# Twenty-four probability scalings of an attention kernel go from VectorE to GpSimd

## Chip, cores and metric

The kernel runs on one core of a Trainium2 chip. The metric is device time in microseconds, as the median of several executions. The engines are named as in the profile: PE is TensorE (matrix multiplication), DVE is VectorE, ACT is ScalarE, POOL is GpSimd, and SP is the engine that issues the DMAs.

## What is computed

The reference is an attention block with a cache of keys and values and with both projections. There are 8 batches of 112 query rows, 32 heads of width 192, and 512 cached positions; the model width is 640, and all arrays are bf16.

```python
B, Sq, D = 8, 112, 640
H, Sk, Dh = 32, 512, 192
q = (x @ wq).reshape(B, Sq, H, Dh).transpose(0, 2, 1, 3)
scores = jnp.einsum("bhqd,bhkd->bhqk", q, k_cache) * (Dh ** -0.5)
p = softmax(scores, axis=-1)
o = jnp.einsum("bhqk,bhkd->bhqd", p, v_cache)
return o.transpose(0, 2, 1, 3).reshape(B, Sq, H * Dh) @ wo
```

The softmax divides each row of exponentials by its sum. The kernel does this division as a multiplication by the reciprocal of the sum, and this multiplication is what the change is about.

## The kernel before

**Tiling.** The 32 heads are worked in 4 rounds of 8, and a round goes through the 8 batches. For one batch a round takes two steps of 4 heads, so there are 64 steps, numbered n = 0 to 63. Within a step the four heads are called i = 0 to 3. The score matrix of one head has 112 rows (on the partitions) and 512 columns.

**One step.** A step passes through these operations. The names are those in the order lists; the lines are those of the profile.

- `Q` (L720, PE; its copy `evQ` at L146 on ACT) makes the projected queries of a group of batches, and `qc` (L761 and L762, DVE) copies parts of them from SBUF to SBUF to where the second half of the array needs them.
- `KT` (L672, PE) transposes the keys of the first batches through PSUM, and `evK` copies them out, one half on ACT (L146) and one on DVE (L147).
- `Sm` and `St` (L773, PE) multiply queries and keys into PSUM banks 0 to 3. They can start only when the `smax` of the step before have emptied these banks.
- `smax` (L830, DVE), once per head, scales the scores, copies them from PSUM to SBUF and keeps the row's minimum of the negated scores. There are three buffers, so `smax` also waits for the `exp` of three heads earlier.
- `exp` (L835, ACT), once per head, makes the exponentials in bf16 in `p_sb` and their row sums.
- `rc` (L847, DVE), once per pair of heads, takes the reciprocal of two row sums.
- `norm` (L839), once per head, multiplies the 112 x 512 bf16 values of `p_sb` in place by the reciprocal. It reads and writes SBUF only. Before the change all 256 of them are on DVE.
- `PT` (L874, PE) transposes the four scaled matrices of the step. It waits for all four `norm`. `evPT` copies the result out, one half on ACT (L146) and the other on DVE (L147).
- `PVt` and `PVm` (L906 and L918, PE) multiply by the values, `evPV` (L146, ACT) copies the result out.
- `O` (L940, PE) multiplies by the output weights, and `oacc` (L954 and L955, DVE) collects it.

**Order.** Nothing is scheduled at run time. Each engine has a list of operations written out by hand (`ORDER_PE`, `ORDER_ACT`, `ORDER_DVE`, `ORDER_POOL`, `ORDER_SP`), and it works through its list strictly in that order. `Plan.run` (lines 35 to 50) emits for each operation the waits on the other operations that it depends on, by counting semaphores: each engine has one, and an operation waits until the count of the engine that produces its input has reached the place of the producer in that engine's list. An operation's engine is the one in whose list its name stands (`number`, lines 23 to 33). So to move an operation it is enough to take its name from one list and to put it into another:

```python
def norm(e, k=k):
    return e.tensor_scalar(p_sb[:, k, :], p_sb[:, k, :], rinv[:, k:k + 1], None, op0=ALU.mult)
...
add("DVE", ("norm", n, i), [("rc", n, j)], norm)
```

`rc` of step n waits for the `norm` of step n - 2, since both use the same reciprocals' place. Heads 0 and 1 depend on the first `rc` of the step (j = 0), heads 2 and 3 on the second (j = 1).

The steps overlap deeply: while one step's scores are made, the step before is scaled and transposed, and an earlier one is multiplied by its values. In the early steps there is additional work: the keys of the first seven batches are transposed on PE and copied out by ACT and DVE, and two groups of queries are projected. Later keys come already transposed by DMA.

`ORDER_POOL` is empty before the change. GpSimd makes the identity matrix at the start (lines 1156 to 1160) and then has nothing to do.

Of the kernel before, what the change touches and what calls it, by code (L numbers as in the profile page):

```python
# [52 lines left out]
def build_mha_kernel(nc, x, k_cache, v_cache, wq, wo, out):  # L53
# [33 lines left out]
    with ExitStack() as es:  # L87
# [145 lines left out]
        def pv_all(n):  # L233
# [191 lines left out]
            ('smax', 1, 3), ('rc', 0, 1), ('evK', 2, 3, 1), ('norm', 0, 2), ('evK', 1, 1, 1), ('evK', 2, 3, 0),  # L425
            ('norm', 0, 3), ('qc', 3), ('evK', 1, 0, 0), ('evK', 1, 3, 1), ('norm', 0, 1), ('norm', 0, 0), ('rc', 1, 0),
            ('evK', 2, 2, 1), ('evK', 2, 0, 1), ('evK', 2, 0, 0), ('smax', 2, 0), ('smax', 2, 2), ('rc', 1, 1),
            ('norm', 1, 1), ('smax', 2, 1), ('norm', 1, 0), ('norm', 1, 3), ('norm', 1, 2), ('smax', 2, 3), ('qc', 4),
            ('evPT', 0, 1), ('smax', 3, 0), ('smax', 3, 1), ('rc', 2, 0), ('rc', 2, 1), ('evPT', 1, 1), ('norm', 2, 2),
            ('evK', 3, 0, 1), ('norm', 2, 0), ('smax', 3, 2), ('smax', 3, 3), ('norm', 2, 1), ('rc', 3, 0),  # L430
            ('evK', 3, 3, 1), ('norm', 2, 3), ('qc', 5), ('smax', 4, 0), ('smax', 4, 1), ('qc', 6), ('norm', 3, 0),
            ('smax', 4, 2), ('smax', 4, 3), ('evPT', 2, 1), ('rc', 3, 1), ('rc', 4, 0), ('norm', 3, 2), ('norm', 4, 1),
            ('norm', 3, 1), ('norm', 3, 3), ('smax', 5, 0), ('evK', 3, 1, 1), ('evPT', 3, 1), ('smax', 5, 1),
            ('smax', 5, 2), ('smax', 5, 3), ('rc', 5, 0), ('rc', 4, 1), ('evK', 3, 2, 1), ('norm', 4, 2), ('smax', 6, 0),
            ('evK', 4, 1, 1), ('smax', 6, 1), ('evK', 4, 2, 1), ('norm', 4, 0), ('evK', 4, 0, 1), ('norm', 4, 3),
            ('evK', 4, 3, 1), ('qc', 8), ('qc', 7), ('rc', 5, 1), ('norm', 5, 2), ('evPT', 4, 1), ('smax', 6, 2),
            ('smax', 6, 3), ('norm', 5, 1), ('evK', 5, 1, 1), ('norm', 5, 3), ('norm', 5, 0), ('smax', 7, 0),
            ('evPT', 5, 1), ('smax', 7, 2), ('rc', 6, 0), ('rc', 6, 1), ('smax', 7, 1), ('smax', 7, 3), ('qc', 9),
            ('norm', 6, 1), ('rc', 7, 0), ('norm', 6, 2), ('norm', 6, 3), ('norm', 6, 0), ('evK', 5, 3, 1), ('smax', 8, 0),
            ('smax', 8, 1), ('smax', 8, 2), ('evPT', 6, 1), ('evK', 5, 0, 1), ('rc', 7, 1), ('smax', 8, 3),  # L440
            ('evK', 5, 2, 1), ('norm', 7, 0), ('norm', 7, 3), ('norm', 7, 1), ('norm', 7, 2), ('smax', 9, 0),
            ('smax', 9, 1), ('rc', 8, 0), ('qc', 10), ('evPT', 7, 1), ('evK', 6, 2, 1), ('rc', 8, 1), ('smax', 9, 2),
            ('norm', 8, 1), ('smax', 9, 3), ('qc', 11), ('norm', 8, 3), ('smax', 10, 0), ('smax', 10, 1), ('norm', 8, 0),
            ('norm', 8, 2), ('rc', 9, 0), ('evK', 6, 3, 1), ('evK', 6, 0, 1), ('smax', 10, 2), ('evPT', 8, 1), ('rc', 9, 1),
            ('norm', 9, 3), ('qc', 12), ('norm', 9, 0), ('norm', 9, 2), ('norm', 9, 1), ('rc', 10, 0), ('smax', 10, 3),
            ('evK', 6, 1, 1), ('evPT', 9, 1), ('norm', 10, 0), ('smax', 11, 0), ('norm', 10, 1), ('smax', 11, 1),
            ('smax', 11, 2), ('rc', 10, 1), ('smax', 11, 3), ('norm', 10, 2), ('norm', 10, 3), ('rc', 11, 0), ('qc', 13),
            ('smax', 12, 0), ('evPT', 10, 1), ('norm', 11, 1), ('rc', 11, 1), ('smax', 12, 1), ('smax', 12, 2),
            ('norm', 11, 2), ('smax', 12, 3), ('norm', 11, 0), ('rc', 12, 0), ('norm', 11, 3), ('qc', 14), ('oacc', 0, 0),
            ('smax', 13, 0), ('norm', 12, 0), ('smax', 13, 2), ('evPT', 11, 1), ('smax', 13, 1), ('rc', 12, 1),  # L450
            ('smax', 13, 3), ('oacc', 0, 4), ('smax', 14, 2), ('norm', 12, 3), ('norm', 12, 1), ('smax', 14, 0),
            ('smax', 14, 1), ('qc', 15), ('norm', 12, 2), ('oacc', 0, 1), ('rc', 14, 0), ('smax', 14, 3), ('qc', 16),
            ('evPT', 12, 1), ('rc', 13, 0), ('norm', 14, 1), ('rc', 13, 1), ('norm', 13, 3), ('oacc', 0, 2), ('rc', 14, 1),
            ('norm', 13, 2), ('norm', 13, 0), ('oacc', 0, 3), ('norm', 14, 2), ('norm', 13, 1), ('smax', 15, 0),
# [96 lines left out]
            ('norm', 63, 3), ('evPT', 62, 1), ('oacc6', 1), ('evPT', 63, 1), ('oacc6', 2), ('oacc6', 0), ('oaccL', 0),  # L551
            ('oaccL', 1)]
        ORDER_POOL = [
]
        ORDER_SP = [
# [608 lines left out]
def bass_standalone__mha_block_cached__near_ridge_kernel(  # L1164
    nc: bass.Bass,
    x: bass.AP,
    k_cache: bass.AP,
    v_cache: bass.AP,
    wq: bass.AP,
    wo: bass.AP,  # L1170
    out: bass.AP,
):
    return build_mha_kernel(nc, x, k_cache, v_cache, wq, wo, out)
# [28 lines left out]
```

## Time and profile before

| what | value |
|---|---|
| median of 3 runs | 438.99 us |
| the three runs | 438.66, 438.99, 440.42 us |
| the profiled execution's own time | 438.76 us |
| its span | 437.0 us |
| granted TensorE clock, mean | 0.995 |
| PE busy | 423.3 us (97%) |
| PE weight loads busy | 290.2 us (66%) |
| DVE busy | 363.1 us (83%) |
| ACT busy | 343.7 us (79%) |
| POOL busy | 0.7 us (0%) |
| DMA traffic | 122.04 MB, mean 279 GB/s |

The span is the time from the first to the last instruction of the profiled execution; its own time holds another 1.76 us around it. PE stands at 97% because its busy time counts pipelined matrix multiplications up to their modelled ends, so PE at 97% is an engine that nearly always has an instruction under way, not one at its peak rate. The shares are means over the whole run. In a row of the timeline the columns are the start in the span, the time taken, the engine, the line, the instruction, its output and input, and how many were merged; a bracket at the end gives the idle time of the engine just before, and who ended it. In a row of the groups the figures behind the first bar are the busy time in us and the mean in ns of one instruction, those behind the second bar the idle time before them.

### The profile page before, as it was taken

How to read it: one execution, taken by the hardware profiler on the slowest of the kernel's cores; microseconds unless marked ns; L12 is line 12 of the kernel's file. 1: busy time of each engine (PE TensorE's matmuls, PEld its weight loads, DVE VectorE, ACT ScalarE, POOL GpSimd, SP SyncE). 2: the span in 40 equal slices, each digit the busy share in tenths (PEclk: the TensorE clock that was granted, in tenths of full speed). 3: DMA queues.
4: the chain of work that ended last, by engine and by line, in shares of the span. 5: the costliest groups of instructions: out<-in, count | busy, mean ns of one | idle time of the engine just before them, and what ended most of it. 6: DMA issues, size and time to landing. Idle time of an engine off the chain costs nothing.

```text
span 437.0 us, 16234 instructions
## 1 busy us (share of the span) xinstructions
PE 423.3 (97%) x6805; PEld 290.2 (66%) x6805; DVE 363.1 (83%) x1169; ACT 343.7 (79%) x770; POOL 0.7 (0%) x6
## 2 busy tenths in 40 slices
PE   7999979999999999999999999999999999999996
PEld 4666756667677566666667666666766666576896
DVE  1479987989699889898999887889799878999872
ACT  2699979998579787988878777887878856985774
POOL 0000000000000000000000000000000000000000
PEclk9999999999999999999999999999999999999999
DMA  7998999999999999999999999999999999999972
GB/s 255 366 354 289 331 358 287 213 289 342 238 288 286 283 256 257 362 263 255 308 240 237 337 255 256 364 352 287 232 242 376 204 247 349 289 252 252 239 201 82
DMA packets 222858, 122.04 MB, mean 279 GB/s; under 512 B 165312, under 2 KB 222784, under 8 KB 222784
## 3 DMA queue, kind: packets, MB, share of 16 engines
q1 hardware_dynamic: 222784, 120.99, 106.6%
q8 instruction: 54, 0.88, 0.8%
q14 instruction: 20, 0.16, 0.1%
HBM read 78.22 MB, written 1.15 MB: 182 GB/s over the span
## 4 chain that ended last, share of the span: by engine, by line
PE 85%; DVE 7%; ACT 4%; DMA 2%; issue 1%; SPq 0%; DVEq 0%; ACTq 0%
PE ps L940 19%; PE ps L720 19%; PE ps L773 18%; PE ps L918 12%; PE ps L906 7%; PE ps L874 5%; DVE s_sb L830 4%; PE ps L672 2%; ACT p_sb L835 2%; DMA wq_sb<-in_wq_dram 2%; DVE p_sb L839 1%; ACT kt L146 1%; PE ps L973 1%; ACT qr L146 1%; DVE pT_sb L147 1%
## 5 line engine op out<-in xcount | busy, mean ns | idle before, releaser
L835 ACT ACTIVATE p_sb<-s_sb,nmx 112x512 bf16<-112x512 f32 x256 | 183.0, 718 | 32.8 <-DVE s_sb L830 25.6
L830 DVE TENSOR_SCALAR_CACHE_REDUCE s_sb<-ps 112x512 f32<-112x512 f32 x256 | 169.2, 683 | 23.3 <-PE ps L773 19.1
L720 PE MATMUL ps<-xT_sb,wq_sb 128*128 128x448 bf16 x480 | 103.2, 356 | 3.1 <-DMA wq_sb<-in_wq_dram 2.1
L773 PE MATMUL ps<-kt,qr 128*128 128x256 bf16 (+1 forms) x512 | 95.6, 273 | 1.1 <-ACT oT_sb L146 0.4
L940 PE MATMUL ps<-oT_sb,wo_sb 128*128 128x448 bf16 (+1 forms) x480 | 93.3, 341 | 0.3 <-DVE pT_sb L147 0.2
L773 PE MATMUL ps<-kt,qh 128*128 128x256 bf16 (+1 forms) x512 | 87.5, 272 | 0.0
L839 DVE TENSOR_SCALAR p_sb<-p_sb,rinv 112x512 bf16<-112x512 bf16 x256 | 81.2, 346 | 1.5
L720 PEld LDWEIGHTS ps<-xT_sb,wq_sb 128*128 128x128 bf16 x480 | 43.1, 98 | 41.9 <-DMA wq_sb<-in_wq_dram 2.8
L940 PEld LDWEIGHTS ps<-oT_sb,wo_sb 128*128 128x128 bf16 x480 | 44.3, 98 | 35.4 <-DVE pT_sb L147 0.8
L146 ACT ACTIVATE oT_sb<-ps 128x672 bf16<-128x672 f32 x64 | 46.1, 725 | 22.3 <-PE ps L918 21.7
L773 PEld LDWEIGHTS ps<-kt,qr 128*128 128x128 bf16 (+1 forms) x512 | 44.3, 96 | 25.7 <-issue 14.3
L146 ACT ACTIVATE qr<-ps 128x448 bf16<-128x448 f32 x96 | 49.7, 541 | 12.8 <-PE ps L720 12.1
L146 ACT ACTIVATE pT_sb<-ps 128x768 bf16<-128x768 bf16 x59 | 47.0, 800 | 10.3 <-PE ps L874 10.2
L918 PE MATMUL ps<-pT_sb,vt 128*128 128x112 bf16 x944 | 54.9, 213 | 0.0
L918 PEld LDWEIGHTS ps<-pT_sb,vt 128*128 128x128 bf16 x944 | 47.4, 98 | 4.1
L835 ACT ACTIVATION_READ_ACCUMULATOR p_sb<-s_sb,nmx 112x1 f32 x256 | 49.7, 194 | 0.0
L773 PEld LDWEIGHTS ps<-kt,qh 128*128 128x128 bf16 (+1 forms) x512 | 43.9, 96 | 6.1
L147 DVE COPY pT_sb<-ps 128x1024 bf16<-128x1024 bf16 x59 | 40.2, 682 | 2.4 <-PE ps L874 1.3
L874 PE MATMUL ps<-ident,p_sb 64*128 64x64 bf16 (+1 forms) x1888 | 37.4, 186 | 0.9 <-DVE p_sb L839 0.5
L874 PEld LDWEIGHTS ps<-ident,p_sb 64*128 64x128 bf16 (+1 forms) x1888 | 33.2, 94 | 6.9 <-DVE p_sb L839 2.6
L906 PE MATMUL ps<-pT_sb,vt 128*64 128x112 bf16 x944 | 32.8, 215 | 1.4 <-DVE s_sb L830 0.5
L906 PEld LDWEIGHTS ps<-pT_sb,vt 128*64 128x64 bf16 x944 | 25.5, 110 | 12.2 <-issue 3.4
(53 smaller groups left out, 228.2 us busy)
## 6 DMA issues: line engine op xcount, KB each, us to landing
vt<-in_v_cache_dram SPq DMA_DIRECT2D x64, 768.0 KB, 6.7
wo_sb<-in_wo_dram SPq DMA_DIRECT2D x8, 960.0 KB, 8.2
wq_sb<-in_wq_dram SPq DMA_DIRECT2D x14, 480.0 KB, 5.7
wo_sb<-in_k_cache_dram SPq DMA_DIRECT2D x6, 768.0 KB, 7.1
accT<-in_k_cache_dram SPq DMA_DIRECT2D x6, 768.0 KB, 7.2
vt<-in_k_cache_dram SPq DMA_DIRECT2D x2, 768.0 KB, 8.5
out_dram<-xT_sb SPq DMA_DIRECT2D x8, 140.0 KB, 2.5
wq_sb<-in_wq_dram SPq DMA_DIRECT2D x1, 960.0 KB, 7.5
```

Source lines behind the costliest of these rows:

```text
L146: return e.activation(dst, src, ACTF.Copy)
L147: return e.tensor_copy(dst, src)
L672: ends = [e.transpose(psb[:, bank + t, y * 64:(y + 1) * 64], kn[i][64 * t:64 * t + 64, 2 * p + u, c * 128:(c + 1) * 128], ident[64 * t:64 ...
L720: mm = e.matmul(ps[:, bank, 0:SG], w, v, start=(dc == 0), stop=(dc == DC - 1))
L773: return e.matmul(ps[:, 2 * j + odd, hs], q, ktb[j][lo:hi, :, blk, h * 128:(h + 1) * 128], start=first, stop=last, skip_group_check=True)
L830: return e.tensor_scalar(s_sb[:, a, :].rearrange("p (e c) -> p e c", e=2), ps[0:SQ, 2 * j:2 * j + 2, h * 256:(h + 1) * 256], -scale, None, ...
L835: return e.activation(p_sb[:, k, :], s_sb[:, a, :], ACTF.Exp, bias=nmx[:, k:k + 1], scale=-1.0, accum_out=rsum[:, k:k + 1])
L839: return e.tensor_scalar(p_sb[:, k, :], p_sb[:, k, :], rinv[:, k:k + 1], None, op0=ALU.mult)
L874: ends.append(e.transpose(psb[:, bank + t, i * w:(i + 1) * w], p_sb[lo:hi, (4 * n + k) % 8, q * 128:(q + 1) * 128], ident[lo:hi, lo:hi]))
L906: mm = e.matmul(ps[64 * h:64 * h + 64, b0 + j, SQ:2 * SQ], vtb[:, h0 + 2 * j + h, d0:d0 + 64], pT(j, h, q), start=(q == 0), stop=(q == 3))
L918: mm = e.matmul(ps[:, b0 + j, 2 * h * SQ:(2 * h + 1) * SQ], vtb[:, h0 + 2 * j + h, d0:d0 + 128], pT(j, h, q), start=(q == 0), stop=(q == 3))
L940: mm = e.matmul(ps[:, bank_of["O", g, m], 0:nc_], wo_sb[:, k, m * 128:(m + 1) * 128], oT_sb[:, g % 2, k, 0:nc_], start=(k == 0), stop=(k = ...
```

## The change

In steps 1 to 12 the `norm` of heads 1 and 3 leave DVE's list, 24 operations in all, and stand in GpSimd's list instead, in order of steps. Nothing else in any list is moved: the operations that are left in DVE's list follow each other as they did. The instruction itself is the same `tensor_scalar`, issued by another engine. `PT` of these steps now waits for two engines, and `rc` of two steps later does, too.

The first of the lines of DVE's list that change (the others lose their `norm` of heads 1 and 3 in the same way), and the new list:

```diff
@@ -425,30 +425,26 @@
             ('norm', 0, 3), ('qc', 3), ('evK', 1, 0, 0), ('evK', 1, 3, 1), ('norm', 0, 1), ('norm', 0, 0), ('rc', 1, 0),
             ('evK', 2, 2, 1), ('evK', 2, 0, 1), ('evK', 2, 0, 0), ('smax', 2, 0), ('smax', 2, 2), ('rc', 1, 1),
-            ('norm', 1, 1), ('smax', 2, 1), ('norm', 1, 0), ('norm', 1, 3), ('norm', 1, 2), ('smax', 2, 3), ('qc', 4),
-            ('evPT', 0, 1), ('smax', 3, 0), ('smax', 3, 1), ('rc', 2, 0), ('rc', 2, 1), ('evPT', 1, 1), ('norm', 2, 2),
-            ('evK', 3, 0, 1), ('norm', 2, 0), ('smax', 3, 2), ('smax', 3, 3), ('norm', 2, 1), ('rc', 3, 0),
-            ('evK', 3, 3, 1), ('norm', 2, 3), ('qc', 5), ('smax', 4, 0), ('smax', 4, 1), ('qc', 6), ('norm', 3, 0),
+            ('smax', 2, 1), ('norm', 1, 0), ('norm', 1, 2), ('smax', 2, 3), ('qc', 4), ('evPT', 0, 1), ('smax', 3, 0),
+            ('smax', 3, 1), ('rc', 2, 0), ('rc', 2, 1), ('evPT', 1, 1), ('norm', 2, 2), ('evK', 3, 0, 1), ('norm', 2, 0),
+            ('smax', 3, 2), ('smax', 3, 3), ('rc', 3, 0), ('evK', 3, 3, 1), ('qc', 5), ('smax', 4, 0), ('smax', 4, 1),
+            ('qc', 6), ('norm', 3, 0), ('smax', 4, 2), ('smax', 4, 3), ('evPT', 2, 1), ('rc', 3, 1), ('rc', 4, 0),
...
         ORDER_POOL = [
-]
+            ('norm', 1, 1), ('norm', 1, 3), ('norm', 2, 1), ('norm', 2, 3), ('norm', 3, 1), ('norm', 3, 3), ('norm', 4, 1),
+            ('norm', 4, 3), ('norm', 5, 1), ('norm', 5, 3), ('norm', 6, 1), ('norm', 6, 3), ('norm', 7, 1), ('norm', 7, 3),
+            ('norm', 8, 1), ('norm', 8, 3), ('norm', 9, 1), ('norm', 9, 3), ('norm', 10, 1), ('norm', 10, 3),
+            ('norm', 11, 1), ('norm', 11, 3), ('norm', 12, 1), ('norm', 12, 3)]
```

The parts of DVE's list before the change that the prediction looks at, by steps: for step 6 `('rc', 6, 0), ('rc', 6, 1), ('smax', 7, 1), ('smax', 7, 3), ('qc', 9), ('norm', 6, 1), ('rc', 7, 0), ('norm', 6, 2), ('norm', 6, 3), ('norm', 6, 0)`; for step 8 `('rc', 8, 0), ('qc', 10), ('evPT', 7, 1), ('evK', 6, 2, 1), ('rc', 8, 1), ('smax', 9, 2), ('norm', 8, 1), ('smax', 9, 3)`; for step 3 `('rc', 3, 1), ('rc', 4, 0), ('norm', 3, 2), ('norm', 4, 1), ('norm', 3, 1), ('norm', 3, 3)`.

More of the change, by code (lines that the diff above doesn't have):

```diff
@@ L432, in build_mha_kernel @@
[L432 to L451, printed above, removed]
+            ('smax', 2, 1), ('norm', 1, 0), ('norm', 1, 2), ('smax', 2, 3), ('qc', 4), ('evPT', 0, 1), ('smax', 3, 0),
@@ new lines, in build_mha_kernel @@
+            ('smax', 3, 1), ('rc', 2, 0), ('rc', 2, 1), ('evPT', 1, 1), ('norm', 2, 2), ('evK', 3, 0, 1), ('norm', 2, 0),
+            ('smax', 3, 2), ('smax', 3, 3), ('rc', 3, 0), ('evK', 3, 3, 1), ('qc', 5), ('smax', 4, 0), ('smax', 4, 1),
+            ('qc', 6), ('norm', 3, 0), ('smax', 4, 2), ('smax', 4, 3), ('evPT', 2, 1), ('rc', 3, 1), ('rc', 4, 0),
+            ('norm', 3, 2), ('smax', 5, 0), ('evK', 3, 1, 1), ('evPT', 3, 1), ('smax', 5, 1), ('smax', 5, 2),
+            ('smax', 5, 3), ('rc', 5, 0), ('rc', 4, 1), ('evK', 3, 2, 1), ('norm', 4, 2), ('smax', 6, 0), ('evK', 4, 1, 1),
@@ new lines, in build_mha_kernel @@
+            ('smax', 6, 1), ('evK', 4, 2, 1), ('norm', 4, 0), ('evK', 4, 0, 1), ('evK', 4, 3, 1), ('qc', 8), ('qc', 7),
+            ('rc', 5, 1), ('norm', 5, 2), ('evPT', 4, 1), ('smax', 6, 2), ('smax', 6, 3), ('evK', 5, 1, 1), ('norm', 5, 0),
+            ('smax', 7, 0), ('evPT', 5, 1), ('smax', 7, 2), ('rc', 6, 0), ('rc', 6, 1), ('smax', 7, 1), ('smax', 7, 3),
+            ('qc', 9), ('rc', 7, 0), ('norm', 6, 2), ('norm', 6, 0), ('evK', 5, 3, 1), ('smax', 8, 0), ('smax', 8, 1),
+            ('smax', 8, 2), ('evPT', 6, 1), ('evK', 5, 0, 1), ('rc', 7, 1), ('smax', 8, 3), ('evK', 5, 2, 1),
@@ new lines, in build_mha_kernel @@
+            ('norm', 7, 0), ('norm', 7, 2), ('smax', 9, 0), ('smax', 9, 1), ('rc', 8, 0), ('qc', 10), ('evPT', 7, 1),
+            ('evK', 6, 2, 1), ('rc', 8, 1), ('smax', 9, 2), ('smax', 9, 3), ('qc', 11), ('smax', 10, 0), ('smax', 10, 1),
+            ('norm', 8, 0), ('norm', 8, 2), ('rc', 9, 0), ('evK', 6, 3, 1), ('evK', 6, 0, 1), ('smax', 10, 2),
+            ('evPT', 8, 1), ('rc', 9, 1), ('qc', 12), ('norm', 9, 0), ('norm', 9, 2), ('rc', 10, 0), ('smax', 10, 3),
+            ('evK', 6, 1, 1), ('evPT', 9, 1), ('norm', 10, 0), ('smax', 11, 0), ('smax', 11, 1), ('smax', 11, 2),
@@ L452, in build_mha_kernel @@
+            ('rc', 10, 1), ('smax', 11, 3), ('norm', 10, 2), ('rc', 11, 0), ('qc', 13), ('smax', 12, 0), ('evPT', 10, 1),
+            ('rc', 11, 1), ('smax', 12, 1), ('smax', 12, 2), ('norm', 11, 2), ('smax', 12, 3), ('norm', 11, 0),
+            ('rc', 12, 0), ('qc', 14), ('oacc', 0, 0), ('smax', 13, 0), ('norm', 12, 0), ('smax', 13, 2), ('evPT', 11, 1),
+            ('smax', 13, 1), ('rc', 12, 1), ('smax', 13, 3), ('oacc', 0, 4), ('smax', 14, 2), ('smax', 14, 0),
             ('smax', 14, 1), ('qc', 15), ('norm', 12, 2), ('oacc', 0, 1), ('rc', 14, 0), ('smax', 14, 3), ('qc', 16),
```

## The prediction

> **What bounds the kernel now.** I read the page first, then the busy times by stretch, then who made TensorE wait.
>
> ```profile
> span 437.0 us, 16234 instructions
> PE 85%; DVE 7%; ACT 4%; DMA 2%; issue 1%; SPq 0%; DVEq 0%; ACTq 0%
> ```
> ```profile
> 36.00:60.00 24.00, 22.17 (x473) 15.76 (x471) 22.96 (x75) 23.28 (x53) 0.00 (x0) 1.00 0.99 329
> 60.00:70.00 10.00, 7.58 (x150) 4.79 (x151) 7.15 (x21) 6.93 (x13) 0.00 (x0) 0.83 1.07 366
> 70.00:86.00 16.00, 15.21 (x325) 10.29 (x324) 14.91 (x48) 15.75 (x37) 0.00 (x0) 1.00 1.00 215
> 86.00:380.00 294.00, 292.19 (x4521) 196.39 (x4520) 257.35 (x834) 235.63 (x540) 0.00 (x0) 1.00 1.15 286
> ```
> ```profile
> PE ps L672 <- issue: 1.8, 1, 1.8
> PE ps L906 <- DVE s_sb L830: 0.5, 1, 0.5
> PE ps L874 <- DVE p_sb L839: 0.5, 2, 0.3
> ```
>
> The columns of the second fence are the length of the stretch and the busy time of PE, weight loads, DVE, ACT and POOL, then the granted clock. From 86 to 380 us TensorE has next to no gap (292.19 of 294.00), and the chain of the whole run is 85% TensorE. DVE work saved there buys nothing. Steps 1 to 8 of the twelve lie in about 36 to 86 us, and only there does TensorE stand still: 24.00 - 22.17 + 10.00 - 7.58 + 16.00 - 15.21 = 5.0 us. The third fence (waits of TensorE in 36 to 86) says for what: 1.8 us is an "issue" gap that no engine caused, and only 0.5 + 0.5 us are on DVE's smax (L830) and norm (L839). DVE and ACT are both over 90% busy in the first and third stretch, so a gain on DVE soon meets ACT. The ceiling is therefore small: about 1 us of direct DVE waits.
>
> **What the change removes.** 24 norms leave DVE's list. Their price is the spacing of neighbours, not their duration.
>
> ```profile
> L839 DVE TENSOR_SCALAR p_sb<-p_sb,rinv 112x512 bf16<-112x512 bf16 x47 | 14.9, 347 | 0.3
> L147 DVE COPY kt<-ps 128x768 bf16<-128x768 bf16 x19 | 10.2, 551 | 4.4 <-PE ps L672 4.4
> L147 DVE COPY pT_sb<-ps 128x1024 bf16<-128x1024 bf16 x12 | 8.2, 684 | 0.3 <-PE ps L874 0.3
> ```
>
> These are DVE's groups in 36 to 115 us. One norm takes 347 ns, but operations overlap by about 0.08 us: three in a row take 0.86 us (third place, below), so (0.86 - 0.35) / 2 = 0.26 us each. 24 x 0.26 = 6.2 us of DVE time go, 0.52 us a step. Most of that lies beside a busy TensorE.
>
> **What it adds: 24 norms on GpSimd.** The trace holds no such operation there. Its nearest rows:
>
> ```profile
> L1158 POOL TENSOR_SCALAR_AFFINE_SELECT ident<-ident 128x128 bf16<-128x128 bf16 x1 | 0.3, 292 | 0.2 <-POOL ident L1156 0.2
> L1156 POOL MEMSET ident<- 128x128 bf16 x1 | 0.2, 204 | 0.3 <-POOLq L1187 0.3
> L1187 POOL MEMSET const-bfloat16-1.0<- 128x1 bf16 x1 | 0.1, 102 | 0.0
> ```
>
> A memset costs 102 ns and (204 - 102) / 127 = 0.80 ns a column; the select, which also reads, (292 - 102) / 127 = 1.50 ns. For 512 columns: 102 + 511 x 0.80 = 0.51 us below, four whole selects (4 x 292 = 1.17 us) above. I take 102 + 511 x 1.50 = **0.87 us**, the slope of the row that reads and writes as a norm does. The Trainium skill's "GPSIMD Engine Reference" (Elementwise — side-by-side cycle accounting) measures 769 ns for 512 elements in a tight loop; by it, an estimate, each norm would be 0.1 us shorter and the sum lower by about as much at each place below. No run here shows it yet.
>
> Two in a row take 1.74 us, and a step lasts some 7 us (steps 3 and 10 transpose at 54.21 and 101.98, below), so the new list keeps up. What it can do to DVE is the open term. Copies out of PSUM cost (684 - 551) / 256 = 0.52 ns a column, so 672 columns would be about 0.50 us; qc, from SBUF to SBUF, does them in 0.33 (the rows at 83.25 and 83.59, below). qc and norm thus read by a wider path than smax and the PSUM copies. GpSimd was idle throughout, so the trace cannot say whether that path stays whole beside it. The ends: no wait at all, or each qc or DVE norm waits out a GpSimd norm in progress. I take the waiting end, as these two operations show an extra path that the other rows lack. The Trainium skill's "SBUF — State Buffer" (Who interferes with whom) says just that: one pair of ports is shared and whoever starts first keeps it for the whole instruction. It speaks against this change.
>
> No wait on DMA or SP is moved. rc of steps 3 to 14 also waits for GpSimd's norms of two steps earlier, and PT for both lists; rc's was done a step ago, PT's is judged below.
>
> **The sum, place by place.** First, step 1:
>
> ```profile
> 38.38 0.16 DVE L847 RECIPROCAL rinv<-rsum 112x2 f32<-112x2 f32 x1
> 38.71 0.68 DVE L830 TENSOR_SCALAR_CACHE_REDUCE s_sb<-ps 112x512 f32<-112x512 f32 x1
> 39.32 0.87 DVE L839 TENSOR_SCALAR p_sb<-p_sb,rinv 112x512 bf16<-112x512 bf16 x3
> 40.11 0.68 DVE L830 TENSOR_SCALAR_CACHE_REDUCE s_sb<-ps 112x512 f32<-112x512 f32 x1
> ```
> ```profile
> 47.24 0.81 ACT L146 ACTIVATE kt<-ps 128x768 bf16<-128x768 bf16 x1 [0.36 <-PE ps L672]
> ```
>
> rc ends at 38.54, GpSimd's norm (1,3) runs from about 38.59 to 39.46 (0.05 us for the signal, as from the end of the norms at 75.51 + 0.86 to the multiplication at 76.43, below). smax now starts at 38.46 and norm (1,0) is ready at 39.07, waits to 39.46, and the next smax starts at 39.98 instead of 40.11: -0.13 us. With no waiting it is 39.59, -0.52, of which ACT, closed up after its 0.36 gap, passes on 0.36. (The pair (2,1), (2,3) then holds GpSimd for 1.74 us from about 43.6 and can hold up DVE's two norms of step 2; its waits for key transposes, 4.4 us in all in the row above, and the 0.52 us of removed norms about cover that.)
>
> Second, the tightest transposition, step 3:
>
> ```profile
> 52.82 0.22 DVE L847 RECIPROCAL rinv<-rsum 112x2 f32<-112x2 f32 x2
> 53.01 1.14 DVE L839 TENSOR_SCALAR p_sb<-p_sb,rinv 112x512 bf16<-112x512 bf16 x4
> 54.21 0.64 PE L874 MATMUL ps<-ident,p_sb 64*128 64x64 bf16 x32 [0.25 <-DVE p_sb L839]
> 55.33 0.58 PE L906 MATMUL ps<-pT_sb,vt 128*64 128x112 bf16 x16 [0.49 <-ACT kt L146]
> ```
> ```profile
> 100.17 0.16 DVE L847 RECIPROCAL rinv<-rsum 112x2 f32<-112x2 f32 x1
> ...
> 101.98 0.63 PE L874 MATMUL ps<-ident,p_sb 64*128 64x64 bf16 x32
> ```
>
> rc (3,1) comes 0.26 earlier (52.7); GpSimd waits out DVE's norm (3,2) to 53.1 and ends near 54.0, so PT can start at 54.05, not 54.21. But TensorE's next wait (0.49 us) is for key copies: nothing. The next tightest is step 10, where rc ends at 100.33 and PT starts at 101.98: 1.6 us of room, above 0.87.
>
> Third, step 6 (the brackets at the end of a row give the idle time before it and its releaser):
>
> ```profile
> 73.00 0.22 DVE L847 RECIPROCAL rinv<-rsum 112x2 f32<-112x2 f32 x2
> 74.46 0.33 DVE L761 COPY qh<-qr 64x672 bf16<-64x672 bf16 x1
> 75.51 0.86 DVE L839 TENSOR_SCALAR p_sb<-p_sb,rinv 112x512 bf16<-112x512 bf16 x3
> 76.43 0.64 PE L874 MATMUL ps<-ident,p_sb 64*128 64x64 bf16 x32 [0.26 <-DVE p_sb L839]
> 84.58 2.07 PE L720 MATMUL ps<-xT_sb,wq_sb 128*128 128x448 bf16 x10 [0.53 <-ACT kt L146]
> ```
>
> GpSimd holds 73.21 to 74.95 with (6,1) and (6,3); qc waits 0.49, then two norms fewer end at 76.34 instead of 76.37: nothing. If (7,1) slips in between DVE's last two norms, the end moves by 0.9 us, of which the PE wait of 0.53 before 84.58 swallows half: +0.4, at even odds +0.2. With no waiting: -0.26.
>
> Fourth, step 8:
>
> ```profile
> 83.25 0.33 DVE L761 COPY qh<-qr 64x672 bf16<-64x672 bf16 x1
> 83.59 0.33 DVE L762 COPY qh<-qr 64x672 bf16<-64x672 bf16 x1
> 84.19 0.69 DVE L147 COPY pT_sb<-ps 128x1024 bf16<-128x1024 bf16 x1 [0.27 <-PE ps L874]
> 86.32 0.68 DVE L830 TENSOR_SCALAR_CACHE_REDUCE s_sb<-ps 112x512 f32<-112x512 f32 x1
> 87.19 0.27 PE L773 MATMUL ps<-kt,qh 128*128 128x256 bf16 x1
> ```
>
> The first qc copy goes ahead, then GpSimd's (8,1) holds 83.58 to 84.45, the second copy comes 0.86 late, 0.27 of it in the idle gap before 84.19: +0.6; one norm fewer before the smax of 86.32 gives -0.26. The score multiplications about 87.1 follow that smax at once, and TensorE hardly rests after (292.19 of 294.00): +0.35.
>
> Sum: -0.13 + 0 + 0.2 + 0.35 = **+0.4 us** on the profiled run's 438.76 (span 437.0 and 1.76 around it): **439.2 us**, 0.2 above the median of 438.99. Steps 9 to 12 add nothing: TensorE is the bound there.
>
> **The rivals.** (a) *GpSimd disturbs nobody*: -0.36 - 0.26 = -0.6, **438.1**. For it: smax and the PSUM copies, most of DVE's time, may be untouched.
>
> (b) *The issue gap shifts away.*
>
> ```profile
> 62.79 0.35 PE L672 MATMUL ps<-ident,accT 64*128 64x64 bf16 x11 [1.77 <-issue]
> 63.07 1.54 PE L720 MATMUL ps<-xT_sb,wq_sb 128*128 128x448 bf16 x5
> 65.50 1.86 PE L720 MATMUL ps<-xT_sb,wq_sb 128*128 128x448 bf16 x5
> 77.00 1.12 PE L720 MATMUL ps<-xT_sb,wq_sb 128*128 128x448 bf16 x5
> ```
>
> TensorE lost 1.77 us there, and another (1.54 - 1.12) + (1.86 - 1.12) = 1.16 in the next two Q lists, at the clock of 0.83. If new waits and times move the gap, up to 2.9 us come back (ACT's idle time in that stretch, 10.00 - 6.93 = 3.1, has room for it): 439.2 - 2.9 = **436.3**. Against: the instructions at that place are the same.
>
> (c) *DVE is held longer than it is relieved* (slower). At 1.17 us a GpSimd norm, the four places become +0.17, 0, up to +0.9 and +0.65, and the pair near 44 us costs ACT another 0.4: +2.1. From 1.2 us on this decides; at 1.5 us, +4: **443**. For: two norms a step already hold DVE's path in reach of nearly each qc.
>
> (d) *A late GpSimd norm makes TensorE stand and its clock drop* as at 62.79: 1.77 + 1.16 = +2.9, **442.1**. Step 3 has 1.2 us between rc and PT, so a norm with its signals beyond that starts it.
>
> **How the numbers follow.** Forecast 0.45, (a) 0.15, (b) 0.10, (c) 0.20, (d) 0.10. A difference under 0.5% (2.2 us) is about what a measurement of this kernel cannot tell from none. Faster: (b), 0.10. Same: forecast and (a), 0.60. Slower: (c) and (d), 0.30. The range leaves out (b) and the upper half of (c): 436.6 to 443.6.
>
> **What would show it.** GpSimd norms near 0.87 us; qc or norm rows of 0.8 us or more where they now take 0.33 to 0.35; the score multiplication of step 10 about 0.3 us later against the row at 87.19; TensorE as gapless as now from there. Norms of 1.2 us, or a PT waiting a microsecond for GpSimd, make it (c) or (d); unchanged DVE rows make it (a); a missing "issue" gap, (b).

## The result and the profile after

Over 20 runs each the changed kernel took 441.6 us (438.99 to 447.18), the kernel before 439.06 us (436.67 to 442.71). The ratio is **1.0051 (95% interval 1.003 to 1.0073)**: about 2.2 us slower (1.3 to 3.2), 441.3 us on the scale of before. The ratio leaves out two slow executions of the changed kernel and is not the quotient of the two medians, here and in the runs below; a difference in us that is given with a ratio is the ratio's. The forecast was 439.2 in a range of 436.6 to 443.6. The result lies in the range and on the side that the sum had (+0.4), but at about five times its size, on the very edge of "within 0.5%". A range of 7 us around a change of 2.2 holds it without telling much.

The profiled execution took 439.09 us, one of the fastest of the 20. These are its first lines, its busy times in the stretches of before, and TensorE's waits in 36 to 86 us (one line number less, since the lists got shorter):

```profile
span 437.0 us, 16248 instructions
PE 79%; DVE 9%; ACT 5%; DMA 4%; issue 2%; SPq 0%; DVEq 0%; ACTq 0%
```
```profile
36.00:60.00 24.00, 21.77 (x492) 15.85 (x488) 22.35 (x69) 23.17 (x53) 13.34 (x9) 1.00 1.03 359
60.00:70.00 10.00, 9.06 (x219) 6.48 (x212) 8.23 (x25) 9.79 (x22) 2.08 (x3) 1.00 0.99 320
70.00:86.00 16.00, 14.05 (x272) 9.06 (x272) 15.28 (x41) 14.38 (x33) 9.67 (x6) 1.00 1.21 224
```
```profile
PE ps L873 <- issue: 1.5, 3, 0.6
PE ps L873 <- DVE p_sb L838: 1.3, 1, 1.3
PE ps L905 <- DVE s_sb L829: 0.5, 1, 0.5
```

The span equals that of before to the tenth, though the medians differ by 2.5 us. One profile against one profile is the wrong comparison here. Before, the "issue" gap at 62.79 us and its slow clock cost TensorE some 3 us (1.77 and 1.16, as the prediction reads them); this execution has no such gap in 60 to 70 (9.06 us busy instead of 7.58, clock 1.00) and has lost as much elsewhere. What the change itself does is in the other rows: TensorE's wait for norm in front of the transposition grew from 0.5 to 1.3 us. (The stretches do not hold quite the same work any more: at 71 us this execution is 3.3 us ahead, the transposition of step 5 at 67.72 instead of 71.02.)

GpSimd's and DVE's groups in 36 to 115 us (GpSimd's over the whole run):

```profile
L838 POOL TENSOR_SCALAR p_sb<-p_sb,rinv 112x512 bf16<-112x512 bf16 x24 | 38.8, 1621 | 71.7 <-DVE rinv L846 71.7
```
```profile
L838 DVE TENSOR_SCALAR p_sb<-p_sb,rinv 112x512 bf16<-112x512 bf16 x23 | 9.9, 448 | 0.2
L761 DVE COPY qh<-qr 64x672 bf16<-64x672 bf16 x11 | 5.9, 534 | 0.1
L760 DVE COPY qh<-qr 64x672 bf16<-64x672 bf16 x12 | 4.4, 370 | 0.4
L829 DVE TENSOR_SCALAR_CACHE_REDUCE s_sb<-ps 112x512 f32<-112x512 f32 x51 | 33.5, 682 | 4.2 <-PE ps L772 3.7 <-ACT p_sb L834 0.5
```

A GpSimd norm takes 1.62 us, not 0.87. The norms left on DVE rose from 347 to 448 ns, the two copies of qc from 329 and 330 to 370 and 534, while smax, which reads PSUM, stayed at 682. That is 23 x 0.10 + 11 x 0.20 + 12 x 0.04 = 5.0 us of holding up, against the 6.2 us of relief that the prediction worked out.

### The profile page after: what moved, and what is told of

It reads as the page before. It is cut to its first block, busy times and chain, and to the rows that moved or that the text cites. A ratio compares the mean times of both kernels' runs of the same rounds, so it can differ in the third digit from the quotient of the medians.

```text
span 437.0 us, 16248 instructions
## 1 busy us (share of the span) xinstructions
PE 422.2 (97%) x6805; PEld 290.4 (66%) x6805; DVE 362.2 (83%) x1145; ACT 343.6 (79%) x770; POOL 39.5 (9%) x30
## 4 chain that ended last, share of the span: by engine, by line
PE 79%; DVE 9%; ACT 5%; DMA 4%; issue 2%; SPq 0%; DVEq 0%; ACTq 0%
PE ps L719 18%; PE ps L772 18%; PE ps L939 17%; PE ps L917 11%; PE ps L905 6%; PE ps L873 5%; DVE s_sb L829 5%; DMA wq_sb<-in_wq_dram 3%; PE ps L671 2%; ACT p_sb L834 2%; DVE p_sb L838 1%; DMA wq_sb<-p_sb 1%; ACT kt L146 1%; PE ps L972 1%; ACT qr L146 1%
## 5 line engine op out<-in xcount | busy, mean ns | idle before, releaser
L829 DVE TENSOR_SCALAR_CACHE_REDUCE s_sb<-ps 112x512 f32<-112x512 f32 x256 | 169.2, 683 | 24.9 <-PE ps L772 19.5
L719 PE MATMUL ps<-xT_sb,wq_sb 128*128 128x448 bf16 x480 | 102.0, 353 | 2.3 <-DMA wq_sb<-in_wq_dram 1.1
L838 DVE TENSOR_SCALAR p_sb<-p_sb,rinv 112x512 bf16<-112x512 bf16 x232 | 76.2, 357 | 1.4
L146 ACT ACTIVATE oT_sb<-ps 128x672 bf16<-128x672 f32 x64 | 46.3, 727 | 20.7 <-PE ps L917 20.2
L838 POOL TENSOR_SCALAR p_sb<-p_sb,rinv 112x512 bf16<-112x512 bf16 x24 | 38.8, 1621 | 71.7 <-DVE rinv L846 71.7
```

The lines of the kernel that those rows point to most:

```text
L146: return e.activation(dst, src, ACTF.Copy)
L719: mm = e.matmul(ps[:, bank, 0:SG], w, v, start=(dc == 0), stop=(dc == DC - 1))
L829: return e.tensor_scalar(s_sb[:, a, :].rearrange("p (e c) -> p e c", e=2), ps[0:SQ, 2 * j:2 * j + 2, h * 256:(h + 1) * 256], -scale, None, ...
```

## The experiments

Two words are used for short below: the *relief* is what DVE no longer has to do, the *company* is GpSimd's work beside DVE. The working theory, that of the **held path**: GpSimd's norm keeps DVE's SBUF-to-SBUF operations waiting, and TensorE feels it in the early steps. The first rival, the **late norm**: TensorE waits for a norm that now takes 1.6 us. The second, formed after the first runs, the **fixed cost**: any GpSimd instruction in these steps costs something through its waits or the instruction stream, whatever its length.

The table gives, for each run, the excess of DVE's norm and qc over their undisturbed lengths in its profile (steps with GpSimd work), the sum of TensorE's waits on DVE in 36 to 118 us in the same profile (rows of its waits view; GpSimd's work of e9 lies behind that stretch), and the ratio to the kernel before. The first two figures are of one execution each.

| run | GpSimd | DVE excess, us | TensorE's waits on DVE, us | ratio, 95% interval |
|---|---|---|---|---|
| kernel before | none | 0 | 1.0 | 1 |
| e12 the same once more | none | 0 | 1.1 | 1.0012 (0.9994 to 1.003) |
| e1 24 norms left out | none | 0 | 1.2 | 1.0014 (0.9987 to 1.0042) |
| e11 48 norms left out | none | 0 | 1.2 | 1.0017 (0.9992 to 1.0043) |
| e10 one column beside | 24 x 0.34 us | 0 | 1.6 | 1.0027 (0.9999 to 1.0055) |
| e9 moved in steps 13 to 24 | 24 x 1.61 | 1.8 | 1.3 | 1.0026 (0.9998 to 1.0055) |
| e5 moved in steps 9 to 12 | 8 x 1.65 | 1.9 | 1.3 | 1.0028 (1.0002 to 1.0054) |
| e6 moved in steps 1 to 8 | 16 x 1.61 | 3.2 | 2.2 | 1.0059 (1.0033 to 1.0085) |
| the change | 24 x 1.62 | 5.0 | 2.2 | 1.0051 (1.003 to 1.0073) |
| e2 beside, all norms kept | 24 x 1.64 | 5.3 | 3.2 | 1.004 (1.0015 to 1.0066) |
| e3 left out and beside | 24 x 1.63 | 3.4 | 0.9 | 1.0043 (1.0015 to 1.0071) |
| e4 half the columns | 24 x 0.97 | 1.3 | 0.9 | 1.0071 (1.0037 to 1.0104) |
| e8 beside, doubled | 48 x 1.60 | 10.9 | 7.0 | 1.012 (1.0082 to 1.0157) |

**e1, the relief alone.** The names of the 24 norms are taken from DVE's list and put nowhere, so heads 1 and 3 of steps 1 to 12 stay unscaled.

```diff
-                add("DVE", ("norm", n, i), [("rc", n, j)], norm)
+                if not (1 <= n <= 12 and i in (1, 3)):
+                    add("DVE", ("norm", n, i), [("rc", n, j)], norm)
```

> Leaves out the scaling of heads 1 and 3 in steps 1 to 12 altogether: 24 norms fewer on VectorE, nothing on GpSimd. This is the pure gain that the change could have. Both theories expect the same: 0.5 to 1 us under the kernel before (438.0 to 438.5), as TensorE bounds the run from 86 us on; a gain of 2 us or more would say that VectorE was on the path far oftener than I read.

Measured 1.0014 (0.9987 to 1.0042), 440.88 us beside 439.42. The expected gain of 0.5 to 1 us does not show: the interval leaves room for 0.13%, or about 1 us if it is read against the middle of e12, the unchanged kernel measured once more (below).

**e11, twice the relief.** All 48 norms of these steps are left out in the same way, and the transposition waits for the reciprocals instead.

> Leaves out all 48 norms of steps 1 to 12, so that VectorE has 12.5 us less to do there and nothing runs on GpSimd. If VectorE's time in these steps is on the path at all, twice the relief shows it: -0.2% to -0.5%. If it is not, as the run without 24 of them says: within 0.2% of the kernel before, and no relief of this size can pay for any company.

Measured 1.0017 (0.9992 to 1.0043), 439.63 us beside 438.69. The busy times in 36 to 118 us, of this run and then of the kernel before:

```profile
36.00:118.00 82.00, 76.78 (x1524) 53.60 (x1521) 61.13 (x183) 72.49 (x163) 0.00 (x0) 1.00 1.08 299
```
```profile
36.00:118.00 82.00, 76.75 (x1486) 52.25 (x1486) 73.18 (x231) 71.43 (x158) 0.00 (x0) 0.98 1.05 296
```

DVE (the third busy time) has 12 us less to do, and TensorE (the first) is as busy as before, to 0.03 us. A DVE at 89% was not the bound, not even in the stretch where TensorE sometimes waits for it. The traces show where a relief goes: in e1 and e11 the transposition of step 6 follows that of step 5 after 4.96 us instead of 5.41, but TensorE then waits 0.29 us for key copies, and from step 5's to step 8's it takes 19.7 us, as before (19.5).

**e2, the company alone.** All norms stay on DVE. GpSimd does 24 multiplications of the same size in a place (zeroed at the start) that is free until `oacc` of group 1; nothing else waits for them.

```diff
-        ORDER_POOL = [
-]
+        ORDER_POOL = [("gd", n, i) for n in range(1, 13) for i in (1, 3)]
...
+                def emit(e):
+                    return e.tensor_scalar(spare, spare, dummy[:, 0:1], None, op0=ALU.mult)
+                add("POOL", ("gd", n, i), [("rc", n, i // 2)] + ([("gd", n, 1)] if i == 3 else [("gd", n - 1, 3)]), emit)
```

> All norms stay on VectorE; 24 multiplications of the same size run on GpSimd on a spare place in SBUF, each after the same reciprocal, and nothing waits for them. Theory of the held path (a GpSimd norm of 1.6 us keeps VectorE's SBUF-to-SBUF operations waiting): 1.5 to 3 us over the kernel before, with rows of 1 us and more among VectorE's norm and qc. Rival of the late norm (the loss comes from TensorE waiting for a norm that takes 1.6 us): no change, within 0.5 us.

Measured 1.004 (1.0015 to 1.0066), 440.7 us beside 439.42. The late norm cannot make this, since nothing in these steps waits for these multiplications; but the interval overlaps that of the unchanged kernel (e12), so how much of this is loss stays unclear. The theory's 1.5 to 3 us hold (1.75), but not its rows of 1 us and more: the longest norm took 0.78 us.

**e8, the company doubled.** Two multiplications after each reciprocal instead of one.

> All norms stay on VectorE; 48 multiplications of 112x512 on GpSimd's spare place in steps 1 to 12, two after each reciprocal: the company of the run with 24 of them, doubled. Theory of the held path (the cost goes with the time that VectorE's norm and qc are held): about 10 us of excess in their rows and twice the cost, +0.8% (3.5 us). Rival (any instruction of GpSimd in these steps costs something fixed, by its waits or its instruction stream): the same +0.4% as with 24.

Measured **1.012 (1.0082 to 1.0157)** in six executions, 444.99 us beside 438.69: 5.3 us by the ratio. TensorE's waits in 36 to 118 us, its largest rows:

```profile
PE ps L873 <- DVE p_sb L838: 3.0, 2, 2.0
PE ps L772 <- DVE s_sb L829: 1.6, 3, 0.6
```

They are those of a DVE that comes late with norm and smax: 7.0 us on DVE in all, 6.0 more than before, against 5.3 us measured. DVE's rows are held 10.9 us, about the 10 expected. That DVE is held and TensorE feels it is shown here, and the late norm has no part in it. A cost that is the same for 24 and 48 would have been 0.4%. A fixed cost for each instruction would double, too; against it stand these waits, and e10.

**e10, company of one column.** The multiplications of e2, of one column.

```diff
-                    return e.tensor_scalar(spare, spare, dummy[:, 0:1], None, op0=ALU.mult)
+                    return e.tensor_scalar(spare[:, 0:1], spare[:, 0:1], dummy[:, 0:1], None, op0=ALU.mult)
```

> All norms stay on VectorE; 24 multiplications of one column only on GpSimd, in the same places and with the same waits as in the run beside the full-sized ones. Held path: no excess in VectorE's rows and no cost, within 0.2%. Rival of the fixed cost: +0.4% again.

Measured 1.0027 (0.9999 to 1.0055), 439.79 us beside 438.69. DVE's norms stayed at 347 ns on average, the longest at 382. The zeroing of the spare place and the waits are those of e2, so what they cost is in this figure. The middle lies between the two expectations and the interval holds both, so this run alone tells nothing apart; e12 below gives the zero to read it by.

**e9 and e5, the move in other steps.** The 24 names of steps 13 to 24 (e9), or the 8 of steps 9 to 12 (e5), stand in GpSimd's list instead.

> The same move of heads 1 and 3, but in steps 13 to 24 instead of 1 to 12, where TensorE has next to no gap. Held path: VectorE is held as often, about 5 us in all, but TensorE's work covers it: within 0.2% of the kernel before. Rival of the fixed cost: +0.4 to 0.5% as in the changed kernel.

> Only the 8 norms of heads 1 and 3 in steps 9 to 12 go to GpSimd. By the prediction these steps add nothing, since TensorE is the bound there: within 0.5 us of the kernel before. If a held VectorE matters here too, a third of the change's loss, +0.7 us.

Measured 1.0026 (0.9998 to 1.0055), 441.07 us beside 438.69, and 1.0028 (1.0002 to 1.0054), 439.96 beside 438.83. e5's interval, 0.1 to 2.4 us, does not tell its two expectations apart. In e9 the ratio alone decides little (the plain medians of all executions lie 0.54% apart), and the profile says more. Its busy times, all of TensorE's waits and DVE's norms in 118 to 200 us:

```profile
118.00:200.00 82.00, 81.76 (x1248) 55.49 (x1247) 67.23 (x207) 64.50 (x149) 38.48 (x24) 1.00 1.14 280
```
```profile
PE ps L719 <- DVE rinv L846: 0.2, 1, 0.2
```
```profile
L838 DVE TENSOR_SCALAR p_sb<-p_sb,rinv 112x512 bf16<-112x512 bf16 x29 | 10.5, 372 | 0.2
```

GpSimd worked 38.48 us there, DVE's norms were held as well (372 ns), and TensorE waited 0.2 us. From the transposition of step 13 to that of step 25 it took 71.61 us, against 71.31 or 71.32 in the kernel before, in e12 and in the change: 0.3 us for 24 moved norms. Where TensorE is the bound, it covers the company nearly whole. DVE was held for 1.8 us only, though, not for the 5 that the expectation named.

**e6, the move in steps 1 to 8 only.**

> Only the 16 norms of heads 1 and 3 in steps 1 to 8 go to GpSimd. By the prediction's place by place sum the whole loss comes from here: +2 us, as in the changed kernel. If the loss comes from all steps alike: +1.5 us.

Measured 1.0059 (1.0033 to 1.0085), 441.28 us beside 438.83: by the middles, the whole of the change's loss; the interval (1.4 to 3.7 us) holds the other expectation's 1.5 us as well. TensorE's waits on DVE are 2.2 us, as in the changed kernel.

**e3, relief and company.** The edits of e1 and e2 together.

> Leaves out the scaling of heads 1 and 3 in steps 1 to 12, and runs the 24 multiplications on GpSimd on a spare place, which nothing waits for: the relief and the company without the wait for the result. Held path: 1 to 2 us over the kernel before, close to the changed kernel. Late norm: 0.5 to 1 us under the kernel before, as in the run with the relief alone.

Measured 1.0043 (1.0015 to 1.0071), 441.79 us beside 439.42. The late norm expected a gain, and none is there, though no result is waited for; the interval overlaps that of e12, so how large the loss is stays unclear. With e8 the late norm is out as the main cause. But TensorE's waits on DVE in the profile, 0.9 us, do not carry it.

**e4, half the columns.** GpSimd's norms take 256 of 512 columns; the other half of these heads stays unscaled.

```diff
-                    return e.tensor_scalar(p_sb[:, k, :], p_sb[:, k, :], rinv[:, k:k + 1], None, op0=ALU.mult)
+                    w = 256 if 1 <= n <= 12 and i in (1, 3) else SK
+                    return e.tensor_scalar(p_sb[:, k, 0:w], p_sb[:, k, 0:w], rinv[:, k:k + 1], None, op0=ALU.mult)
```

> The changed kernel with GpSimd's norms cut to 256 of the 512 columns (the other half of these heads stays unscaled), so that one takes about 0.85 us, the size that the prediction took. Held path: between 0 and 0.8 us over the kernel before (the prediction's +0.4), about 2 us under the changed kernel. Late norm: a gain of about 0.5 us, as no transposition would wait at that size.

Measured 1.0071 (1.0037 to 1.0104), 442.34 us beside 439.42: both theories missed. A norm took 0.97 us, DVE was held a quarter as long as in the change, TensorE waited for DVE no more than before, and yet the run is not faster than the change (the intervals overlap). The profiled execution shows more "issue" gaps in 36 to 118 us, 3.9 us; but e9 has 4.4 us of them there, with no GpSimd work in that stretch, and 0.7 us of e4's execution are lost between the transpositions of steps 13 and 25, when GpSimd is done. The cause of this loss stays open.

**e7, what a GpSimd multiplication costs.** Twelve operations at the very start, two of each form, each after the one before.

> The kernel before with twelve multiplications or copies on GpSimd at the very start, on a spare place, two of each form: 512, 256 and 128 bf16 columns by a scalar per row, 512 bf16 by a constant, 256 f32 by a scalar per row, a copy of 256 bf16. If the price goes by columns: 1.56, 0.83, 0.47 us, and f32 of 256 columns about 0.8. If it is a fixed price of the scalar per row: the constant form is much cheaper, near 0.87.

GpSimd's timeline (start, time of both, instruction, form; the constant form has no second input):

```profile
1.98 3.22 POOL L1047 TENSOR_SCALAR accT<-accT,dmy_act 112x512 bf16<-112x512 bf16 x2
5.29 1.94 POOL L1048 TENSOR_SCALAR accT<-accT,dmy_act 112x256 bf16<-112x256 bf16 x2
7.33 1.30 POOL L1049 TENSOR_SCALAR accT<-accT,dmy_act 112x128 bf16<-112x128 bf16 x2
8.71 3.06 POOL L1050 TENSOR_SCALAR accT<-accT 112x512 bf16<-112x512 bf16 x2
11.87 1.94 POOL L1051 TENSOR_SCALAR accT<-accT,dmy_act 112x256 f32<-112x256 f32 x2
13.88 0.86 POOL L1052 COPY accT<-accT 112x256 bf16<-112x256 bf16 x2
```

It goes by columns: 1.61, 0.97 and 0.65 us, that is (1.61 - 0.65) / 384 = 2.5 ns a column. The scalar per row matters little (1.53 with a constant), the type not at all (256 columns of f32 as of bf16), and a copy costs less than half (0.43 instead of 0.97). This kernel was run once, at 439.69 us.

**e12, the zero.** The kernel before, unchanged.

> The kernel before, unchanged, measured as the others were. It gives the zero of these comparisons: five kernels that by the held path should cost nothing or gain (the two reliefs, the move in steps 9 to 12, the move in steps 13 to 24, the one-column company) came out at +0.14 to +0.28%. If the control is at 0 within its interval and clearly below them, a fixed cost of about 0.2% in any changed kernel is left; if it lies among them, they are zeros, and only what stands above it is a cost.

Measured 1.0012 (0.9994 to 1.003), 439.21 us beside 438.44. It lies just below the five, and all their intervals overlap with its own. So the reliefs, the later moves and the one-column company are zeros as far as this measurement goes. Clear of its interval stand e4, e6 and e8; the change touches it (1.003 and 1.003); e2 and e3 stand above it only by their middles. Of the change's 0.51% some 0.1% may be the zero's.

## Why the prediction came out as it did

- **The bound and the ceiling: right, and even too kind.** "DVE work saved there buys nothing" for the later steps is what e9 shows. The prediction still saw about 1 us to be won in steps 1 to 8. In e1 and e11 no gain shows, and if there is one, it is no more than about 1 us.

- **The price of a GpSimd norm: wrong.** The step that failed is "I take 0.87 us". It measures 1.62, above even the upper end of 1.17 that was drawn from four selects. The slope of the select (1.50 ns a column) was that of a lighter operation; a multiplication has 2.5. The Trainium skill's "GPSIMD Engine Reference" (Elementwise — side-by-side cycle accounting) has 769 ns for 512 elements in a tight loop: the trace has twice that for this operation, and the measurement decides.

- **The form of the wait: wrong too, to the other side.** The walk let DVE wait out the whole GpSimd norm. At the first place, GpSimd's row of the changed kernel and then DVE's:

```profile
38.16 1.56 POOL L838 TENSOR_SCALAR p_sb<-p_sb,rinv 112x512 bf16<-112x512 bf16 x1 [1.10 <-DVE rinv L846]
```
```profile
38.58 0.68 DVE L838 TENSOR_SCALAR p_sb<-p_sb,rinv 112x512 bf16<-112x512 bf16 x2
39.17 0.68 DVE L829 TENSOR_SCALAR_CACHE_REDUCE s_sb<-ps 112x512 f32<-112x512 f32 x1
```

Two DVE norms start and end inside one GpSimd norm (38.16 to 39.72) and take 0.68 us instead of 0.61. The next smax comes 0.59 us after the first norm, not after a full wait. Here the change won: TensorE's first multiplication by values, before and then in the changed kernel:

```profile
43.37 0.24 PE L906 MATMUL ps<-pT_sb,vt 128*64 128x112 bf16 x1 [0.55 <-DVE s_sb L830]
```
```profile
42.50 0.58 PE L905 MATMUL ps<-pT_sb,vt 128*64 128x112 bf16 x16 [0.48 <-DVE s_sb L829]
```

Of these 0.87 us, 0.48 had been gained before 36 us already (by an earlier load), and 0.39 here. Other traces bear this out: from the start of rc (1,1) to this multiplication it is 4.99 us in the kernel before, e12, e5, e7 and e9, where DVE keeps all norms of step 1 and GpSimd is idle, and 4.59 both in the change and in e1. So GpSimd's norm cost nothing at this place: that is rival (a)'s 0.36, not the -0.13 of the sum.

- **Step 3: right.** rc (3,1) ends at 51.79, GpSimd works from there with DVE's norm in between, and the transposition follows it:

```profile
51.88 3.27 POOL L838 TENSOR_SCALAR p_sb<-p_sb,rinv 112x512 bf16<-112x512 bf16 x2 [4.47 <-DVE rinv L846]
```
```profile
53.71 0.62 PE L873 MATMUL ps<-ident,p_sb 64*128 64x64 bf16 x32 [0.28 <-issue]
```

The wait is 0.28 us, before it was 0.25. The first of the two GpSimd norms ends at 53.61, 0.10 us before the transposition. The profile puts the gap down to "issue"; the times fit a wait for GpSimd.

- **Step 6: the case given even odds came, and it is the one loss of size that the trace shows.**

```profile
69.97 4.74 POOL L838 TENSOR_SCALAR p_sb<-p_sb,rinv 112x512 bf16<-112x512 bf16 x3 [4.90 <-DVE rinv L846]
```
```profile
71.18 0.54 DVE L760 COPY qh<-qr 64x672 bf16<-64x672 bf16 x1
71.73 0.72 DVE L761 COPY qh<-qr 64x672 bf16<-64x672 bf16 x1
72.49 0.17 DVE L846 RECIPROCAL rinv<-rsum 112x2 f32<-112x2 f32 x1
72.57 1.41 DVE L838 TENSOR_SCALAR p_sb<-p_sb,rinv 112x512 bf16<-112x512 bf16 x2
```
```profile
74.04 0.64 PE L873 MATMUL ps<-ident,p_sb 64*128 64x64 bf16 x32 [1.33 <-DVE p_sb L838]
```

Three GpSimd norms stand in a row, and every qc copy and norm that DVE does meanwhile takes 0.54 to 0.77 us. TensorE waits 1.33 us instead of 0.26: +1.07, where the sum had +0.9 before cover, in even odds. The cover did not come: the wait for key copies that was to swallow half of it is still 0.53 us. The same wait for DVE's norms stands in e6 (1.33), e2 (1.22) and e8 (1.96).

- **Step 8: not there.** The second copy of qc took 0.73 us instead of 0.33, not 0.86 late, and TensorE's score multiplications did not wait for smax: that +0.35 fell away.

So in this execution the four places come to -0.39 + 0 + 1.07 + 0 = +0.7 us, against +0.4 predicted and 1.2 us more of TensorE's waits on DVE in 36 to 118. That these two sums lie so close is in part luck: the price was too low by almost half, the form of the wait too strict, and the two errors worked against each other. The measured +2.2 us (1.3 to 3.2) is more than either. 0.5 us of it may be the zero of the comparison.

Laid side by side, the fourteen traces (one execution each) place the loss better than any one of them. From the transposition of step 5 to that of step 8 TensorE took 19.5 to 19.7 us in seven of the eight executions without GpSimd's long multiplications there (e5 20.2), and 20.3 to 20.9 in five with it (the change 20.83), 23.7 in e8. From step 2's to step 3's it took 5.4 to 5.9 us without (e9 6.3) and 6.3 to 7.2 with it (the change 6.51, before 5.74, e12 5.80). In the change these two stretches and the gain at step 1 come to about +1.6 us; 0.6 of it is an "issue" gap inside step 2's transposition, where e5, e7, e9 and e12 have gaps of 0.3 to 0.8 us, too. In e3 and e4 the excess is there, too, but as "issue" gaps (1.5 and 0.9 us between steps 5 and 8) and not as waits on DVE. Such gaps fall without GpSimd's work as well (0.7 us there in e5), so whether GpSimd's work makes them is not shown, and that part of the cause stays open.

- **The rivals.** (a), no disturbance, is out by DVE's rows and by e8. (b) cannot be judged from one profile: the gap was 1.77 us before and, at the same place, 1.35 us in e12, and it was missing in the changed kernel's profile; it varies by execution, and the two identical spans fit that. (c), DVE held longer than relieved, is nearest to the mechanism, but its condition did not come (held 5.0 us, relieved 6.2): the change loses because the relief brings next to nothing. And its price was wrong: at 1.5 us it said +4, and 1.62 gave +2.2, as DVE is held for a part of the time only. (d) did not come: the granted clock is 1.00 in all three stretches above.

## What to carry to other kernels

Before work is taken off a busy engine, leave it out altogether and time that: here 12 us less on an engine that was 89% busy brought nothing that could be measured, so any cost of the new place was pure loss. An engine's rate for one operation is not had from its rate for another: the multiplication was 1.7 times as slow a column as the nearest row. And where two executions of the same kernel lie 2.3 us apart at the transposition of step 13 (125.88 in the kernel before, 123.63 in e12), two profiles with the same span prove nothing; a rerun of the unchanged kernel says how small a ratio can be read.

## What the runs showed of the hardware

In the changed kernel 18 of the 48 norms and qc copies of DVE in 36 to 119 us lay wholly inside stretches of GpSimd norms. The longest took 0.77 us, 6 of them no more than 0.36: GpSimd holds DVE up in two parts of its operation, not through it. DVE norms that start 0.09 to 0.47 us after GpSimd's start mostly end 0.83 us after it, in the change, e2 and e3 alike (832, 832 and 832 ns for those at 0.28); those that start at 0.48 to 0.98 mostly run undisturbed; those at 1.03 to 1.25 all end at 1.71 where the GpSimd norm took its shortest, 1.56 us (seven of them), and mostly at 1.78 to 1.91 where it took longer. So a DVE norm of 0.35 waits until about 0.48 in the first part and about 1.36 in the second, of a GpSimd norm of 1.56. The Trainium skill's "SBUF — State Buffer" (Who interferes with whom) has the pair of ports kept for the whole instruction and the other engine fully blocked. The trace agrees on who disturbs whom (norm and qc are slowed; smax takes 682 ns beside 683 in the kernel before, and DVE's two kinds of PSUM copies 549 and 686 beside 551 and 684) and does not agree on "whole": the longest wait in any of these runs is about 0.46 us of 1.56 (a norm of 0.80 in e8).
